# Moving batch 1's q loads ahead of a weight load, and turning q through the banks of the second channel matmul

## The chip, the cores and the metric

The kernel runs on one core of one Trainium2 chip. The metric is the device time of one execution in microseconds (us). Each run is labelled fast or slow: slow when it is over 1.5% above the fastest of its kernel, which comes with a lower granted TensorE clock. A ratio is the mean time of one kernel's fast runs over that of the other's of the same rounds, so it is not quite the ratio of the medians quoted beside it. It stands with its 95% interval.

## The reference

A linear attention with a cosine reweighting, then a mixer over tokens and one over channels; eight batches, 576 tokens, eight heads of 64.

```python
def phi(x, c, s):
    r = np.maximum(x, 0.0)
    return np.concatenate([r * c, r * s], axis=-1)
q_p, k_p = phi(q, cos_w, sin_w), phi(k, cos_w, sin_w)
kv  = np.einsum('bhsf,bhsd->bhfd', k_p, v)
num = np.einsum('bhsf,bhfd->bhsd', q_p, kv)
den = np.einsum('bhsf,bhf->bhs', q_p, np.sum(k_p, axis=2))[..., None] + 1e-06
x = (num / den)                                  # heads side by side: (batch, 576, 512)

xt = x.transpose(0, 2, 1)
u  = x + (np.maximum(xt @ w_tok1, 0.0) @ w_tok2).transpose(0, 2, 1)
return u + np.maximum(u @ w_ch1, 0.0) @ w_ch2    # 512 -> 1536 -> 512
```

## The kernel before

Inputs are loaded in float32, turned into bf16 features ("qfeat", "kfeat") and multiplied on TensorE. The q features have to be transposed ("turned") before they can multiply kv: either on TensorE through a PSUM bank (`qturn_mm`, `qturn_out`), or by a transposing DMA (`qturn_dma`). Likewise u is transposed for the first channel matmul (`mlp1`), whose result goes into the second (`mlp2`, twelve steps of k in three parts). In the names below, `num` multiplies the turned q features with kv, `x_out` divides that by the sum in its last column and so frees `num`'s bank (a bank is the piece of PSUM that a matmul writes), `b1` is the first token matmul, `u_mm` the second, and the tail is the last 64 of the 576 tokens. A "w_ch2 cast" turns a staged piece of the second channel weight into bf16. All tiles of SBUF are handed out one behind the other in the order in which they are named:

```python
raw = {n: [sb(f"{n}_raw{i}", [P, H, NJ, D], F32) for i in range(2)] for n in "qkv"}
# ... kp, qp, vb, qpT, kv_sb, x_sb, x_tl, x_tc ...
rden = [sb(f"rden{i}", [P, 2, HH], F32) for i in range(2)]
B1 = [sb(f"B1_{i}", [P, NT, Dm], BF16) for i in range(2)]
u_sb = [sb(f"u_sb{i}", [P, T, Dm], F32) for i in range(2)]      # also w_ch staging
u_tl = sb("u_tl", [P, B // 2, Dm], F32)                         # also w_ch staging
# ... u_bf, u_bt, uT, uTt, h1T (also w_tok staging), res (also w_ch staging), ...
```

Three places are changed. The head (batch 0) ends so:

```python
for c in (2, 3):
    uT_x(c, bank_u[c])
for c in (2, 3):
    uT_h(0, c, bank_u[c])                 # needs the relu of the second B half
    uT_out(0, c, bank_u[c], (A, V)[c - 2])
for mi in (0, 1):
    mlp1_part(0, mi, bank_h[mi], (0, 1))  # needs only uT blocks 0 and 1
```

The middle, between batch 0 and the loop, mixes batch 1's attention with batch 0's second channel matmul:

```python
wc2_load(0, SY)
load(1, q, "q", (SY, SY))
for i in (1, 2):
    wc2_load(i, SY)
# ...
for j in range(NJ):
    kv(1, j)
for t in range(3):
    p(0, t)                               # 12 matmuls of mlp2 part 0
for j in range(NJ):
    qfeat(1, j, V, A if j != 3 else V)
turn1(0, V)
turn1(1, A)
p(0, 3)
turn1(2, V)
turn1(3, A)
num1(0)
p(1, 0)
# ... num1 and p(1, ...) in turn, then b1, then p(2, ...)
```

The loop has a plan by steps for the batches that follow; in that of its first round:

```python
for n in range(2):
    put(13 + n, u_step, b, n)
    put(15 + n, uturn_step, b, n)                # u cast, transposing DMA
for j in range(3):
    put((12, 13, 15)[j], qfeat, f, j, A, A)
    put((12, 13, 17)[j], qturn_dma, f, j)        # transposing DMA of q
put(8, q_load, 4)
put(9, v_load, 4)
```

## Time and profile before

| | before |
|---|---|
| time, median of 3 runs | 262.38 us (261.79 to 262.49) |
| span of the profiled run | 259.7 us |
| TensorE busy | 248.5 us |
| VectorE, ScalarE, GpSimd busy | 190.2, 155.4, 101.0 us |

The lines on the bound, the gaps and the chain of waits are in the prediction. Two more views of this kernel are needed below. The first is TensorE's timeline behind kv of batch 1 (start, length, engine and line, operation, output and input, shapes, count): the channel matmul at 37.19 fills the time in which q is awaited, without a gap ahead of the first turn at 39.78.

```profile
35.97 1.38 PE L190 MATMUL psA<-vb,kp 128*128 128x65 bf16 x40
37.19 2.76 PE L337 MATMUL psM<-w_ch,h1T 128*128 128x512 bf16 x11
39.78 1.06 PE L176 MATMUL psA<-ident,qp 128*128 128x128 bf16 x16
```

The second is the DMA view of the stretch from 20 to 44 us, in which the staged weights and batch 1's inputs come in back to back: how many packets moved, how much, how fast.

```profile
DMA packets 6483, 9.37 MB, mean 390 GB/s; under 512 B 193, under 2 KB 4113, under 8 KB 6480
```

### The profile page before, as it was taken

Reading aid. Unit: us, or ns where it says so; the run is one execution under the profiler, and the core shown is the slowest. Engines: PE = TensorE matmul, PEld = TensorE weight load, DVE = VectorE, ACT = ScalarE, POOL = GpSimd, SP = SyncE. Lnnn points to the kernel's source line nnn. Section 1 sums busy time; section 2 is a strip of 40 time slices with the busy share of each in tenths; the row PEclk is TensorE's granted clock in tenths of the full one; section 3 lists DMA queues with packets and bytes.
Section 4 is the critical chain, followed back from the end, with each engine's and each line's share of the span. In section 5 each row is a group of like instructions: output and inputs, shape, how many; then the busy total and the mean of one; then the engine's idle time right before and its main releaser. Section 6 shows DMA issues by size and latency. Waiting matters only on the chain.

```text
span 259.7 us, 5679 instructions
## 1 busy us (share of the span) xinstructions
PE 248.5 (96%) x2098; PEld 157.7 (61%) x2110; DVE 190.2 (73%) x452; ACT 155.4 (60%) x259; POOL 101.0 (39%) x176
## 2 busy tenths in 40 slices
PE   7698999999999999999999999999999999999994
PEld 2465456455568545865596558755865576486483
DVE  5893767799989479949994999399939763653563
ACT  4663586885999458945883589357934443513510
POOL 5188467261007910392039303820381054044041
PEclk9999999999999999999999999999999999999999
DMA  6999999999999999999999997976290034004004
GB/s 192 368 372 390 390 388 386 332 257 260 302 356 214 182 341 354 180 224 297 350 184 186 375 282 153 192 256 120 66 232 36 0 81 180 4 0 156 8 0 163
DMA packets 79948, 57.18 MB, mean 220 GB/s; under 512 B 48177, under 2 KB 74929, under 8 KB 79921
## 3 DMA queue, kind: packets, MB, share of 16 engines
q1 hardware_dynamic: 76128, 47.26, 67.8%
q0 software_dynamic: 2560, 8.39, 9.5%
q10 hardware_dynamic: 1232, 1.18, 1.4%
q8 instruction: 16, 0.26, 0.4%
q14 instruction: 12, 0.09, 0.1%
HBM read 35.85 MB, written 9.44 MB: 174 GB/s over the span
## 4 chain that ended last, share of the span: by engine, by line
PE 63%; DMA 3%; DVE 2%; issue 1%; DVEq 0%
PE psM L319 26%; PE psM L386 24%; PE psA L239 4%; PE psA L257 3%; DMA qpT<-qp 3%; PE psA L214 2%; PE psA L190 2%; DVE qp L147 1%; PE psA L298 1%; PE psA L386 1%; DVE res L413 0%; DVE res L438 0%; DVE res L424 0%; DVE res L409 0%; DVE res L428 0%
## 5 line engine op out<-in xcount | busy, mean ns | idle before, releaser
L319 PE MATMUL psM<-uT,w_ch 128*128 128x512 bf16 x368 | 88.0, 379 | 0.6 <-DVE res L438 0.6
L331 ACT ACTIVATE h1T<-psM 128x512 bf16<-128x512 f32 x93 | 55.5, 597 | 39.7 <-PE psM L319 38.0
L404 POOL TENSOR_TENSOR res<-res,u_sb 128x256 f32<-128x256 f32 x42 | 32.2, 797 | 96.2 <-DVE res L409 95.8
L319 PEld LDWEIGHTS <-w_ch 128*128 128x128 bf16 x416 | 38.1, 98 | 40.4 <-issue 0.8
L386 PEld LDWEIGHTS <-h1T 128*128 128x128 bf16 x288 | 27.3, 98 | 5.8
L145 ACT ACTIVATE kp<-k_raw,sin_t 128x512 bf16<-128x512 f32 (+1 forms) x45 | 28.4, 669 | 1.2 <-DMA k_raw<-in_k_dram 1.2
L145 ACT ACTIVATE qp<-q_raw,sin_t 128x512 bf16<-128x512 f32 (+1 forms) x40 | 26.6, 681 | 0.1
L386 PE MATMUL psM<-w_ch,h1T 128*128 128x256 bf16 x192 | 25.0, 273 | 0.0
L163 POOL CAST vb<-v_raw 128x512 bf16<-128x512 f32 (+1 forms) x38 | 20.7, 588 | 11.0 <-DMA v_raw<-in_v_dram 10.6
L386 PE MATMUL psM<-w_ch_t,k_raw 128*128 128x256 bf16 x186 | 23.6, 273 | 0.0
L386 PEld LDWEIGHTS <-k_raw 128*128 128x128 bf16 x204 | 19.7, 98 | 5.0 <-issue 1.2
L214 PEld LDWEIGHTS <-qpT 128*128 128x128 bf16 x320 | 14.8, 98 | 10.3 <-issue 1.6
L361 DVE TENSOR_TENSOR k_raw<-h1T 128x512 bf16<-128x512 bf16 (+2 forms) x31 | 11.1, 360 | 12.3 <-ACT h1T L331 11.5
L230 DVE TENSOR_TENSOR x_sb<-psA,rden 128x512 bf16<-128x512 f32 x28 | 19.4, 691 | 1.0
L262 DVE TENSOR_TENSOR u_sb<-psA,x_sb 128x1024 f32<-128x1024 f32 x16 | 19.4, 1216 | 0.1
L147 DVE TENSOR_SCALAR kp<-k_raw,cos_t 128x512 bf16<-128x512 f32 (+1 forms) x40 | 17.5, 468 | 1.8 <-DMA k_raw<-in_k_dram 1.8
L147 DVE TENSOR_SCALAR qp<-q_raw,cos_t 128x512 bf16<-128x512 f32 (+1 forms) x37 | 16.2, 469 | 2.0 <-DMA q_raw<-in_q_dram 2.0
L226 DVE TENSOR_SCALAR rden<-psA 128x8 f32<-128x8 f32 x35 | 5.7, 164 | 15.4 <-PE psA L214 15.1
L257 PE MATMUL psA<-B,w_tok 128*128 128x512 bf16 x64 | 16.4, 379 | 0.0
L214 PE MATMUL psA<-kv_sb,qpT 128*128 128x65 bf16 x280 | 14.3, 193 | 0.7 <-DMA qpT<-qp 0.4
L239 PE MATMUL psA<-x_sb,w_tok 128*128 128x512 bf16 x49 | 14.0, 379 | 0.6 <-DVE x_sb L230 0.2
L200 ACT CAST kv_sb<-psA 128x520 bf16<-128x520 f32 x7 | 4.2, 603 | 16.7 <-PE psA L190 16.7
(139 smaller groups left out, 391.6 us busy)
## 6 DMA issues: line engine op xcount, KB each, us to landing
out_dram<-res POOLq DMA_DIRECT2D x32, 256.0 KB, 4.9
k_raw<-in_k_dram SPq DMA_DIRECT2D x7, 640.0 KB, 8.2
v_raw<-in_v_dram SPq DMA_DIRECT2D x7, 640.0 KB, 9.9
q_raw<-in_q_dram SPq DMA_DIRECT2D x7, 640.0 KB, 11.2
k_raw<-in_k_dram SPq DMA_DIRECT2D x7, 512.0 KB, 6.6
v_raw<-in_v_dram SPq DMA_DIRECT2D x7, 512.0 KB, 10.0
q_raw<-in_q_dram SPq DMA_DIRECT2D x7, 512.0 KB, 8.7
u_sb<-in_moe_w_ch_dram SPq DMA_DIRECT2D x2, 1024.0 KB, 10.3
```

Of the source, the lines that this page charges most:

```text
L145: eng.activation(out_ap, in_ap, AF.Relu, bias=0.0, scale=s)
L147: eng.tensor_scalar(out_ap, in_ap, scalar1=s, scalar2=0.0, op0=ALU.mult, op1=ALU.max)
L163: eng.tensor_copy(out_ap, in_ap)
L214: nc.tensor.matmul(dst, w, kv_sb[:, h, 0:E1], start=True, stop=True, skip_group_check=True)
L230: nc.vector.tensor_mul(dst.rearrange("p (g h d) -> p g h d", g=2, h=HH), n[:, :, :, 0:D], rb)
L239: nc.tensor.matmul(b1_ps[b][mi], w1[:, jw, mi * P:(mi + 1) * P], x, start=(j == 0), stop=(j == T))
L257: nc.tensor.matmul(ps[:, half, :], w2[:, ki, 2 * c + half, :], B1[b % 2][:, ki, :], start=(ki == 0), stop=(ki == NT - 1))
L262: nc.vector.tensor_add(u_sb[b % 2][:, 2 * c:2 * c + 2, :], ps, x_sb[:, 2 * c:2 * c + 2, :])
L319: nc.tensor.matmul(ps.rearrange("p (t k) -> p t k", k=P), wc1[:, ki, mi * P:(mi + 1) * P], src[:, :, ki, :], start=(ki == 0), stop=(ki == ...
L331: eng.activation(h1T[:, mi, :], ps, AF.Relu)
L386: nc.tensor.matmul(m[tt][:, tt, :], a[:, c, tt * P:(tt + 1) * P], w[:, c, :], start=(pr < 4 and c == 0 and (tt == 0 or own)), stop=(c == N ...
L404: G.tensor_add(c[:, t, :], s[:, t, :], u[:, t, :])
```

## The change

The intent: bring q in before the weights that are wanted later, turn q earlier through the banks that the second channel matmul owns anyway, and fill the wait for the head's last relu with matmuls that don't need it. One small piece moves a multiply from VectorE to ScalarE, and gets a small tile of its own for the reciprocals, so that it need not wait for the shared one. Lastly one transposing DMA of q goes from step 13 to 17 of the loop's first round. The diff, cut to its core:

```diff
     rden = [sb(f"rden{i}", [P, 2, HH], F32) for i in range(2)]
+    r_t = sb("rden_t", [P, 1, HH], F32)
     B1 = [sb(f"B1_{i}", [P, NT, Dm], BF16) for i in range(2)]
...
+        if eng is nc.scalar:                      # in x_half: the tail's multiply
+            for h in range(HH):
+                eng.activation(dst[:, 0, h, :], n[:, 0, h, 0:D], AF.Copy, bias=0.0, scale=r[:, 0, h:h + 1])
+            return
...
+    tail_b = psK[1].rearrange("p (g n) -> p g n", g=1)
+    num_half(1, pairs[2], tail_b)                 # ahead of the first B half
...
+    for mi in (0, 1):
+        mlp1_part(0, mi, bank_h[mi], (0, 1))
     for c in (2, 3):
         uT_h(0, c, bank_u[c])
         uT_out(0, c, bank_u[c], (A, V)[c - 2])
-    for mi in (0, 1):
-        mlp1_part(0, mi, bank_h[mi], (0, 1))
...
-    wc2_load(0, SY)
     load(1, q, "q", (SY, SY))
-    for i in (1, 2):
+    for i in range(3):
         wc2_load(i, SY)
...
-    for ki in (0, 2):
+    for ki in (0, 3):
         wc2_cast(ki, G)
...
-    for ki in (1, 3):
-        wc2_cast(ki, A)
-    kv_out(1, A)
...                                                # turn1 now writes the banks mps of mlp2:
-        qturn_out(j, qturn_mm(j), eng)
+        qturn_out(j, qturn_mm(j, mps[j] if j < 4 else nextA()[:, 0, :]), eng)
...
-    for t in range(3):
-        p(0, t)
-    for j in range(NJ):
-        qfeat(1, j, V, A if j != 3 else V)
+    qfeat(1, 0, V, V)
+    qfeat(1, 1, V, A)
+    kv_out(1, A)
+    qfeat(1, 2, V, A)
     turn1(0, V)
     turn1(1, A)
+    for ki in (1, 2):
+        wc2_cast(ki, V)
+    qfeat(1, 3, V, A)
+    turn1(2, V)
+    qfeat(1, 4, V, A)
+    num1(0)
+    p(0, 0)
...                                                # num, turn and p(0, ...) in turn; p(1, ...) around b1
-                put((12, 13, 17)[j], qturn_dma, f, j)
+                put((12, 17, 17)[j], qturn_dma, f, j)
```

More of the change, by code (lines that the diff above doesn't have):

```diff
@@ L170, in qturn_dma, with qturn_mm @@
                                     in_=qp[j].rearrange("p h a d -> p (h a d)"))
-    def qturn_mm(j):
-        ps = nextA()
-        t = ps[:, 0, :].bitcast(BF16).rearrange("p (h t) -> p h t", h=H)
+    def qturn_mm(j, bank):
+        t = bank.bitcast(BF16).rearrange("p (h t) -> p h t", h=H)
         for h in range(H):
@@ L502, in num_half, with x_half @@
                 num_mm(ps[:, i, h * E1:(h + 1) * E1], 0, HH * hf + h, j)
-    def x_half(hf, js, ps, b, stages=(0, 1, 2)):
+    def x_half(hf, js, ps, b, stages=(0, 1, 2), eng=None, slot=None):
         m = len(js)
         n = ps[:, 0:m, 0:HH * E1].rearrange("p g (h e) -> p g h e", h=HH)
-        r = rden[(js[0] // 2) % 2]
+        r = rden[(js[0] // 2) % 2] if slot is None else slot
         rm = r[:, 0:m, :]
@@ L731 @@
         num_half(1, pairs[i], num_b[i])
-    x_half(1, pairs[0], num_b[0], 0, (0,))
-    x_half(1, pairs[0], num_b[0], 0, (1,))
-    x_half(1, pairs[0], num_b[0], 0, (2,))
-    x_half(1, pairs[1], num_b[1], 0, (0,))
-    x_half(1, pairs[1], num_b[1], 0, (1,))
+    tail_b = psK[1].rearrange("p (g n) -> p g n", g=1)
+    num_half(1, pairs[2], tail_b)
+    for st in range(3):
+        x_half(1, pairs[0], num_b[0], 0, (st,))
+    for st in range(2):
+        x_half(1, pairs[2], tail_b, 0, (st,), slot=r_t)
+    for st in range(3):
+        x_half(1, pairs[1], num_b[1], 0, (st,))
     b1_half(0, range(NJ), psK[0], 0)
     b1_half_out(0, psK[0], 0, A)
+    x_half(1, pairs[2], tail_b, 0, (2,), A, r_t)
     for c in range(2):
         uT_x(c, psT[c])
-    num_half(1, pairs[2], num_b[2])
-    x_half(1, pairs[1], num_b[1], 0, (2,))
-    x_half(1, pairs[2], num_b[2], 0)
     for c in range(2):
@@ L823, in num1 @@
         x_out(1, j)
-    for t in range(3):
-        p(0, t)
-    for j in range(NJ):
-        qfeat(1, j, V, A if j != 3 else V)
+    qfeat(1, 0, V, V)
+    qfeat(1, 1, V, A)
+    kv_out(1, A)
+    qfeat(1, 2, V, A)
     turn1(0, V)
     turn1(1, A)
-    p(0, 3)
-    turn1(2, V)
-    turn1(3, A)
-    num1(0)
-    p(1, 0)
-    num1(1)
-    p(1, 1)
-    turn1(4, A)
-    num1(2)
-    p(1, 2)
+    for ki in (1, 2):
[5 more added lines that the diff above has]
+    p(0, 0)
+    turn1(3, A)
+    num1(1)
+    p(0, 1)
+    turn1(4, A)
+    p(0, 2)
+    num1(2)
+    p(0, 3)
     num1(3)
-    p(1, 3, (0, 3))
     num1(4)
-    t_sum(0)
     for bb in range(2):
         tail_copy(bb)
-    p(1, 3, (3, 4))
+    p(1, 0)
+    for mi in range(NT):
+        b1(1, mi)
+        b1_out(1, mi, (A, V)[mi])
+        p(1, 1 + mi)
+    t_sum(0)
     for j in range(2):
@@ L850 @@
         qturn_dma(2, j)
-    for mi in range(NT):
-        b1(1, mi)
-        b1_out(1, mi, (A, V)[mi])
     load(3, k, "k", (SY, SY))
@@ L859 @@
         load(3, src_of[n], n, (SY, SY))
+    p(1, 3)
     p(2, 0)
```

## The prediction

> **What bounds the kernel now.** I read the page first: busy shares, then the slices.
>
> ```profile
> PE 248.5 (96%) x2098; PEld 157.7 (61%) x2110; DVE 190.2 (73%) x452; ACT 155.4 (60%) x259; POOL 101.0 (39%) x176
> DMA  6999999999999999999999997976290034004004
> ```
>
> TensorE is busy for 248.5 of 259.7 us, so all that can be won without removing matmuls is 11.2 us of idle TensorE. Most of that lies before 15 us (11.05 busy of 15.00), which the change leaves alone. The change adds and removes no matmul; it can only move TensorE's gaps. The DMA row says that transfers are queued until about 156 us, so landing times matter too.
>
> Second, the timeline of TensorE alone, from 15 to 60 us, for the places where one row's last start does not run into the next row.
>
> ```profile
> 22.28 0.39 PE L545 MATMUL psN<-ident,x_sb 128*128 128x128 bf16 x4
> 23.23 0.39 PE L550 MATMUL psK<-w_tok,B 128*128 128x512 bf16 x1 [0.56 <-ACT B L539]
> ...
> 41.54 1.06 PE L176 MATMUL psA<-ident,qp 128*128 128x128 bf16 x16
> 42.93 0.40 PE L214 MATMUL psA<-kv_sb,qpT 128*128 128x65 bf16 x8 [0.34 <-DVE qpT L163]
> ...
> 48.54 1.02 PE L239 MATMUL psA<-x_sb,w_tok 128*128 128x512 bf16 x4 [0.19 <-DVE x_sb L230]
> ```
>
> In steady state one 512-column matmul issues every 0.216 us (1.03 us for four, less the 0.38 us that one takes, over three), a 128-column transpose every 0.056 us, a 65-column matmul every 0.030 us. With those steps the gaps are: about 0.3 us near 19.7, 0.5 near 22.5 to 23.2 (0.7 in the records; one record of that group is missing), 0.5 at 42.4, and 0.14, 0.35 and 0.18 between 45.5 and 49.6. That is near 2.0 us in all. From 24 to 36 us TensorE has none.
>
> Third, the chain of waits that ended last, where it meets the loop over the later batches:
>
> ```profile
> 85.26 0.61 DVE res L438
> 85.87 0.12 issue
> 85.98 1.35 PE psM L319 x6
> 87.33 7.04 DMA qpT<-qp
> 94.37 0.05 issue
> 94.42 0.42 PE psA L214 x8
> ```
>
> After 94.42 the chain is TensorE almost without a break to the end. So the end is set by when TensorE gets past two stops: 0.7 us before 85.98 (last start before it 85.24) and 0.55 us before 94.42, where batch 3's last q block is awaited from a transposing DMA. The profile gives the first stop to the VectorE add at L438, but that reads another bank than the one this first matmul writes (the source rotates four banks; bank one was read at 83.98). The view of tile uT from 74 to 96 us has a better candidate:
>
> ```profile
> L272 SPq DMA_TRANSPOSE uT<-u_bf x2: 1238/1292/1347, 81.4 to 82.8; - x2
> DMA to landing us min/median/max: 3.1/3.4/3.6
> ```
>
> The second of these is issued at 82.8 and lands 3.1 us later or more: 85.9, which is when TensorE starts. I take the transposed u, not the add, for the releaser.
>
> [...]So swapping two loads on SyncE's queue swaps their landings and adds no bytes. The trace agrees: loads are issued about 11 us before they land, one behind the other (q's halves 11.2 us median between 17 and 45 us, at 389 GB/s). [...]The trace has 0.71 us for 512 columns with a pointer scale[...]. [...]512 columns take 0.69 us from PSUM and 0.48 or 0.42 from SBUF.[...]
>
> **The change, part by part.**
>
> *Tail x of batch 0 (near 18 to 21 us).* The four tail matmuls move ahead of the first B half: they delay it by 4 x 0.030 = 0.12 us, and the ScalarE relu behind it (19.30 now) and the first u matmuls (19.95 now) by the same. Two small VectorE instructions (0.16 and 0.18) move ahead of x of pair 1, which has slack: it lands near 20.3, needed at 21.2. The 0.42 us multiply on VectorE becomes four ACTIVATEs of 64 columns[...]. Their bank is wanted again at 21.1. So +0.12 us and no win here.
>
> *First channel matmul ahead of the last u matmuls (22.5).* Four 512-column matmuls, 4 x 0.216 = 0.86 us, go where TensorE waits for the relu, whose halves are done near 23.3. They cover the 0.5 us gap whole. The copies of the last two u blocks (0.6 and 0.69 us) then have 0.86 us of matmuls to hide behind instead of 1.73, and just fit. Net of the 0.12: TensorE reaches the next stage **0.4 us** earlier.
>
> *q before w_ch2, and the turns.* q(1) lands at 38.1 now. A w_ch2 part is 1.05 MB, 2.6 us at 389 GB/s. So q lands near 35.5 and w_ch2's first part at 38.1. VectorE can use q only behind its last relu of the first channel matmul (36.25 to 36.94 now, 0.4 earlier then). Going through VectorE in its order: relu to 36.55; four features at a step of 0.40 to 38.1; first turn copy 0.69 to 38.8; two w_ch2 casts to 39.6; feature, turn copy, feature to 41.1; five x_out of 1.05 to 1.13 each to about 47.1. TensorE against it: kv ends 36.8, then nothing until q block 0 is ready (37.4): 0.65 idle. Turns to 38.8; first num at 38.85; channel matmul part 0 waits for the casts (0.35 idle, two pieces); turn 3 waits for its features (0.2); turn 4 needs the bank that x_out(0) frees at 42.1 (0.35); num 4 waits for x_out(2) (0.3). After it the b1 matmuls are interleaved with the second part, which covers most of the old 0.53 there. I get part 2 starting near 51.05 against 50.87 now: idle of 1.6 in place of 1.0. So this part *gives back* **0.6 us**: the old order had 12 independent channel matmuls (2.6 us) to run behind kv while q was awaited, the new one has none.
>
> *The transposing DMA of batch 3's block 1 from step 13 to 17.* It is issued at about 78.4 now and holds SyncE to 81.29, although u's first half is cast at 79.1. Behind the u transposes instead, u goes out at 79.1 and 81.3, and lands near 84.5, before TensorE wants it (85.24). The first stop, **0.7 us**, goes. The q blocks follow back to back from 82.6, four at 1.3 us, the last issued near 86.7 (87.33 now), before or beside the four output stores that start at 85.82. It should land 0.3 to 0.8 us earlier, but it is wanted 0.7 + 0.55 us earlier. I count **0.3 us** of the second stop as won.
>
> Sum: -0.4 + 0.6 - 0.7 - 0.3 = -0.8 us.
>
> **Rivals.** (a) *The middle is as good as its intent:* no idle behind kv, all 1.0 us of old gaps gone. For it: q is 2.6 us earlier and no turn waits for DMA any more. Against it: VectorE's queue, 10.5 us of work from 36.55 to 47.1 without a hole. It would make -0.4 - 1.0 - 1.0 = -2.4, so 260.0. (b) *Everything before 94.42 is absorbed by the DMA:* if the last q transpose lands at 94.4 again, what TensorE wins earlier becomes a longer wait there, and the time stays 262.4. For it: DMA is queued through 95 us, and earlier transposes took up to 7.0 us to land. Against: the u transposes landed within 3.1 to 3.6 us of issue, so the queue is short there. (c) *VectorE becomes the bound in the middle more than I have it:* each slip in its chain counts whole; 1 us more there gives 262.6. (d) *The w_ch2 load hides nothing:* its first part lands at 38.1, first wanted at 39.1, so a late landing by over 0.5 us stalls part 0. Slower by over 2% would need 5 us of new TensorE idle; only a serialisation that I have not seen gives that.
>
> **Range and chances.** From 262.38 I take 0.8, and a little more for (a), since ScalarE and VectorE work freed from the wait for q may be used better than my walk has it: 261.4 us. The spread is (a) at 260.0, (b) and (c) near 262.5; the runs of before spread 0.7. 8 in 10: 260.4 to 262.5. Over 2% is 5.2 us, more than the sum of all gaps after 15 us: faster 0.01, same 0.97, slower 0.02.
>
> **What would show it right or wrong.** The gap before the last u matmuls is gone, and TensorE starts the loose u matmuls of psA (27.34 now) near 26.95. q features start at 36.5 on VectorE, no wait for q's DMA; w_ch2's first cast near 38.1. TensorE idles 0.5 us or more behind kv and part 2's first matmul is at 50.5 to 51.5. The first matmul of batch 2's channel step starts without the 0.7 us stop. The num of batch 3's block 4 still waits, if briefly, for its DMA. The prediction is wrong if the middle has under 0.5 us of idle, or if the u transpose is not what ended the first stop (then it stays, with L438 ahead of it), or if block 4 of q lands later than 94.

From the trace of before: the 0.71 us is that of an ACTIVATE on ScalarE, the 0.69 and the 0.48 or 0.42 us are VectorE's. The cut estimate for the tail x on ScalarE was only the argument that it ends before its bank is wanted again at 21.1; in the trace after, the four ACTIVATEs take 0.93 us and end at 21.05.

## The result, and the profile after

The changed kernel takes 265.38 us at the median of four runs (fast ones 265.08, 265.29 and 265.46; one slow run of 270.29). Before, with one more run, is at 262.09. The ratio is 1.0128 [1.0088, 1.0167]: slower by 1.3%, inside the 2% band, but 2.9 us above the upper end of the predicted range. The profiled runs, both fast, are 261.47 (before) and 265.29 (after).

The page's busy row of the kernel after shows where the loss is not: VectorE, ScalarE and GpSimd are as busy as before to 0.3 us. TensorE shows 2.0 us more for the same 2098 matmuls. Its ends are modelled, and a wait inside a row can count as busy: kv's 40 matmuls take 1.54 us below and 1.38 before.

```profile
PE 250.5 (95%) x2098; PEld 157.9 (60%) x2110; DVE 190.5 (72%) x453; ACT 155.1 (59%) x261; POOL 101.1 (38%) x176
```

I cut both traces at points that every variant has and took the time between them. "Head" runs from the first turn on TensorE to the first u matmul of L257; the next part from there to kv of batch 1 is 8.63 us in all kernels; "middle" runs from kv of batch 1 to the loop; "rounds 1, 2" are the loop's first two rounds, in which stop one and stop two of the prediction lie; "rest" runs to the last matmul.

| us | first turn at | head | middle | rounds 1, 2 | rest |
|---|---|---|---|---|---|
| before | 7.80 | 19.54 | 21.24 | 55.85 | 142.74 |
| after | 8.02 | 19.01 | 23.32 | 56.45 | 143.69 |
| difference | +0.22 | -0.53 | +2.08 | +0.60 | +0.95 |

The differences sum to the 3.32 us between the two last matmuls. The first column varies from run to run (7.6 to 9.1 over all kernels) and lies ahead of the change.

**Head, as predicted.** TensorE's timeline of the kernel after: the channel matmuls at 22.71 fill the wait for the relu, and the u matmuls of L257 start at 27.03 (predicted 26.95).

```profile
22.71 1.03 PE L326 MATMUL psT<-uT,w_ch 128*128 128x512 bf16 x4
23.79 0.38 PE L554 MATMUL psK<-w_tok,B 128*128 128x512 bf16 x1
...
27.03 1.03 PE L257 MATMUL psA<-B,w_tok 128*128 128x512 bf16 x4
```

**Middle, much worse.** The same timeline behind kv; brackets give the idle time just before a row and what ended it. The first turn waits for q's features, turn 4 for the bank that x_out frees. The wait at 40.55 is put down to a DMA into u_sb, but that one lands only at 42.28; the first weight cast, on GpSimd from 39.63 to 40.50, ends just before 40.55, so I take that cast for the releaser.

```profile
35.66 1.54 PE L190 MATMUL psA<-vb,kp 128*128 128x65 bf16 x40
37.90 1.09 PE L176 MATMUL psM<-ident,qp 128*128 128x128 bf16 x16 [0.70 <-DVE qp L148]
39.20 0.62 PE L176 MATMUL psM<-ident,qp 128*128 128x128 bf16 x8 [0.21 <-ACT qp L146]
39.66 0.41 PE L214 MATMUL psA<-kv_sb,qpT 128*128 128x65 bf16 x8
40.55 1.13 PE L337 MATMUL psM<-w_ch,h1T 128*128 128x512 bf16 x4 [0.48 <-DMA u_sb<-in_moe_w_ch_dram]
...
43.61 0.61 PE L176 MATMUL psA<-ident,qp 128*128 128x128 bf16 x8 [0.22 <-DVE x_sb L230]
```

Part 2 starts near 52.64 (eight steps of 0.216 behind 50.91), outside the 50.5 to 51.5 that the prediction named.

**Stop one gone, stop two grown.** Later in that timeline: round 2 starts at 87.05 with no wait. It is 28.07 us behind round 1's start, before it was 28.77, so the predicted 0.7 came. But two num groups, not one, now wait for q's transposing DMA, and longer.

```profile
87.05 2.75 PE L319 MATMUL psM<-uT,w_ch 128*128 128x512 bf16 x12
...
94.27 0.42 PE L214 MATMUL psA<-kv_sb,qpT 128*128 128x65 bf16 x8 [0.28 <-DMA qpT<-qp]
...
96.37 0.42 PE L214 MATMUL psA<-kv_sb,qpT 128*128 128x65 bf16 x8 [0.82 <-DMA qpT<-qp]
```

**Transfers are slower from the start.** The DMA view of 20 to 44 us of the kernel after has 372 GB/s where before had 390, though the queue was full in both (the DMA row of that stretch has the digit 9 in all 40 slices):

```profile
DMA packets 6031, 8.92 MB, mean 372 GB/s; under 512 B 177, under 2 KB 3584, under 8 KB 6028
```

In 24 us that is 0.45 MB less, or 1.2 us at that rate. Indeed q lands at 36.87 us where I had 35.5, and the first part of w_ch2 at 39.58 where I had 38.1. Nothing in the prediction's reasoning moves a byte more, so the question for the experiments is: why did transfers slow down?

**Theories.** (A) *Placement.* The tile `rden_t` takes 32 bytes per partition (16 of them used) ahead of B1, so all tiles behind it (u, res, h1T, transposed u, and the weights staged in them) start 32 bytes further on. I read the addresses out of the build: before, the DMA targets among them start at multiples of 256; after, all at 32 above one. That this slows the transfers was my supposition at this point; e1 to e3 test it. (B) *Order.* The new order of loads and of engine work makes the transfers collide, wherever the tiles lie. (C) *The middle is VectorE-bound* beyond what I had walked, and the DMA is a bystander.

My count of the trace's packets between 20 and 44 us, median nanoseconds by size:

```
              2048 B   1024 B   1280 B     start of B1, mod 256   raw q, k, v, mod 256
before          84       46       56              0                     192
after           88       49       60             32                     192
```

### The profile page after: what moved, and what is told of

Same layout as the page of the kernel before. It is cut to its first block, busy times and chain, and to the rows that moved or that the text cites. A ratio compares the mean times of both kernels' runs of the same rounds, so it can differ in the third digit from the quotient of the medians.

```text
span 263.2 us, 5683 instructions
## 1 busy us (share of the span) xinstructions
PE 250.5 (95%) x2098; PEld 157.9 (60%) x2110; DVE 190.5 (72%) x453; ACT 155.1 (59%) x261; POOL 101.1 (38%) x176
## 4 chain that ended last, share of the span: by engine, by line
PE 51%; DMA 3%; DVE 1%; ACT 1%; issue 0%; ACTq 0%
PE psM L319 24%; PE psM L386 18%; DMA uT<-u_bf 3%; PE psA L239 3%; PE psA L257 3%; PE psA L214 2%; PE psA L190 1%; ACT u_bf L267 1%; PE psA L386 1%; ACT kp L146 0%; PE psA L298 0%; DVE u_tl L303 0%; DVE res L413 0%; DVE kp L148 0%; DVE res L409 0%
## 5 line engine op out<-in xcount | busy, mean ns | idle before, releaser
L319 PEld LDWEIGHTS <-w_ch 128*128 128x128 bf16 x416 | 38.0, 97 | 41.1 <-issue 1.4
L257 PE MATMUL psA<-B,w_tok 128*128 128x512 bf16 x64 | 16.4, 379 | 0.0
L245 ACT ACTIVATE B<-psA 128x512 bf16<-128x512 f32 x13 | 7.8, 597 | 14.0 <-PE psA L239 13.9
L214 PE MATMUL psA<-kv_sb,qpT 128*128 128x65 bf16 x280 | 14.3, 193 | 1.2 <-DMA qpT<-qp 1.1
```

Source lines behind the costliest of these rows:

```text
L214: nc.tensor.matmul(dst, w, kv_sb[:, h, 0:E1], start=True, stop=True, skip_group_check=True)
L257: nc.tensor.matmul(ps[:, half, :], w2[:, ki, 2 * c + half, :], B1[b % 2][:, ki, :], start=(ki == 0), stop=(ki == NT - 1))
L319: nc.tensor.matmul(ps.rearrange("p (t k) -> p t k", k=P), wc1[:, ki, mi * P:(mi + 1) * P], src[:, :, ki, :], start=(ki == 0), stop=(ki == ...
```

## The experiments

Line numbers in views of edited kernels are off by the lines added. Times are medians of all runs in us, slow ones included, this kernel's first, then those of before in the same rounds.

### Placement alone

**e1: the kernel before, with an unused tile of 32 bytes ahead of B1.**

```diff
+    sb("pad", [P, 8], F32)
     B1 = [sb(f"B1_{i}", [P, NT, Dm], BF16) for i in range(2)]
```

> The kernel before with nothing changed but an unused 32-byte tile ahead of B1, so that B1, u_sb, u_tl, u_bf, uT, uTt, h1T and res start 32 bytes later, as they do in the changed kernel (there the new tile rden_t does it). Theory A (the shift slows DMA into and out of these tiles): q of batch 1 lands over 1 us later than 38.05, w_ch2's 2048-byte packets take 87 to 89 ns where they took 84, and the time is 263.3 to 265. Theory B (the shift costs nothing, the changed kernel loses by its new order alone): 262.1 within 0.6, q lands at 38.0 within 0.4.

Measured: 265.21 against 262.88, 1.0116 [1.0055, 1.0178]. One tile that nothing reads or writes costs, within the noise, what the whole change costs. (One of the four runs, 267.79, has a clock of 0.990; without it, and without before's 264.11 at 0.993, the ratio of the means is 1.0098.) The engines are as busy as before (VectorE 189.9 us, ScalarE 155.7, GpSimd 100.8), so it isn't they that the shift slows. The DMA view of the same stretch matches the kernel after, and so do the packets (88, 48, 60 ns):

```profile
DMA packets 6047, 8.92 MB, mean 372 GB/s; under 512 B 179, under 2 KB 3616, under 8 KB 6044
```

The view of waits (waiter, releaser: total, times, longest, us) of e1 shows where it surfaces in the loop: stop one is longer, not shorter.

```profile
PE psM L320 <- DMA uT<-u_bf: 1.6, 2, 1.5
PE psA L215 <- DMA qpT<-qp: 0.7, 1, 0.7
```

**e3: the same with 64 bytes**, to see whether it is the number 32 or the loss of the 256-byte start (`sb("pad", [P, 16], F32)`).

> As e1 with 64 bytes in place of 32: B1 and the tiles after it start at a multiple of 64, not of 256. If what matters is the 256-byte start, as slow as e1 (263.3 to 265 by theory A); if it is a 64-byte start, 262.1 within 0.6 with packets of 84 ns. Theory B: 262.1 in any case.

Measured: 265.92 against 262.88, 1.0120 [1.0083, 1.0157]; packets 88, 48, 60 ns. 64 is as bad as 32.

**e2: the kernel after, with 224 bytes behind `rden_t`**, so that B1 and all behind it start at multiples of 256 again.

```diff
     r_t = sb("rden_t", [P, 1, HH], F32)
+    sb("pad", [P, 56], F32)
```

> The changed kernel with 224 bytes of unused padding behind rden_t, so that B1 and all tiles after it start at a multiple of 256 bytes again. Theory A: 262.0 within 0.8, q of batch 1 lands near 35.5 and w_ch2's first part near 38.0, and the waits for transposed u at 115 and 194 us are gone. Theory B: 265.3 within 0.5, landings as in the changed kernel (36.87 and 39.58).

Measured: 263.84 against 262.88, 1.0013 [0.9967, 1.0058]; packets 84, 46, 59 ns; q lands at 35.75 and w_ch2's first part at 38.22, as theory A had it. All code of the change is in it, and by the ratio it is the kernel before again in time. Two points of theory A's text were missed: 263.84 lies above its 261.2 to 262.8 (before, too, ran 0.8 us longer in these rounds), and of the two waits for transposed u the one at 115 us is gone, the one at 194 still has 0.55. With e1: 1.0116 x 1.0013 = 1.0129, and the kernel after has 1.0128. So theory A holds for the bulk of the loss, and B doesn't explain it: the order is the same in e2, and e1 has the old one. The rate is back too:

```profile
DMA packets 6419, 9.30 MB, mean 388 GB/s; under 512 B 191, under 2 KB 4042, under 8 KB 6416
```

A caution: e2's trace is of a run of 263.98, the slowest of its three fast ones, while the profile of before is of a quick one (261.47). These two traces differ by more than the rounds do (the table below), so I take the sizes from the rounds and the places from the traces.

### The parts of the change alone

**e14: the head part alone**, on the kernel before: `mlp1_part` for banks 0 and 1 ahead of the last u matmuls.

```diff
+    for mi in (0, 1):
+        mlp1_part(0, mi, bank_h[mi], (0, 1))
     for c in (2, 3):
         uT_h(0, c, bank_u[c])
         uT_out(0, c, bank_u[c], (A, V)[c - 2])
-    for mi in (0, 1):
-        mlp1_part(0, mi, bank_h[mi], (0, 1))
```

> The kernel before with the head part alone, tiles where they were. The head wins 0.4 to 0.6 us at the first u matmuls. If the wait for q of batch 1 (it lands at 38.05 at the earliest, and the old middle starts its features with it) takes that up, the loop starts as before and the time is that of before, ratio 0.999 to 1.001. If it passes through: 0.998.

Measured: 262.17 against 262.48, 0.9981 [0.994, 1.0023], not clear of the noise by itself. The trace has it in place: the head takes 18.99 us instead of 19.54.

**e15: the q transpose from step 13 to 17 alone** (`(12, 17, 17)` for `(12, 13, 17)`).

> The kernel before with the last part alone, the q transpose of batch 3's block 1 from step 13 to 17. By e4's profile: the first stop (0.7 us) goes, the second grows from 0.55 to 2.3 us: ratio 1.002 to 1.005. By e5 against e2 (it was 0.3 per cent slower to undo it): 0.996 to 0.998.

Measured: 263.05 against 262.48, 0.9995 [0.9948, 1.0041]. No change, to within half a per cent. By itself the move doesn't remove stop one, as these two lines of its waits show: the transposed u has to go out behind a q transpose that holds SyncE until 79.89, goes out at 79.98 and 83.05 and lands at 86.67, later than before (85.85).

```profile
PE psM L319 <- DMA uT<-u_bf: 1.2, 1, 1.2
PE psA L214 <- DMA qpT<-qp: 0.9, 1, 0.9
```

**e4: both of these together.**

> The kernel before with only two parts of the change, and no new tile: the first channel matmul ahead of the last u matmuls, and the q transpose of batch 3's block 1 from step 13 to 17. My walk of the kernel before gave 0.5 us for the first (without the tail's 0.12) and 0.7 to 1.2 for the second: 260.4 to 260.9. If early savings are absorbed by the wait for the last q transpose near 94 us: 262.1 within 0.4.

Measured: 262.38 against 262.88, 0.9974 [0.9937, 1.0011]. Its view of waits shows that stop one is down to 0.2 us, but the step change doesn't shorten stop two, which is 2.3 us here; so the forecast of 260.4 to 260.9 was missed:

```profile
PE psA L214 <- DMA qpT<-qp: 2.3, 1, 2.3
```

**e6: the middle part alone**, with the order of loads, the new turns and the new mix of matmuls from the change, and no new tile.

```diff
-    wc2_load(0, SY)
     load(1, q, "q", (SY, SY))
-    for i in (1, 2):
+    for i in range(3):
         wc2_load(i, SY)
...                    # turns, features, casts and p(...) as in the change
```

> The kernel before with the middle part alone: q loaded ahead of w_ch2, the new order of features, turns and channel matmuls. No new tile, so all tiles stay where they were. By my walk this part costs 0.6 us of TensorE idle before the loop; in e2 it cost 1.35 us from kv to the first matmul of the loop. If TensorE's time before the loop counts, 262.7 to 263.8 (ratio 1.002 to 1.006). If the DMA queue alone sets the stop near 94 us, the loop starts 0.6 to 1.4 us late and the time is that of before within 0.3.

Measured: 263.55 against 262.58, 1.0042 [0.9996, 1.0087]. In its trace the middle takes 22.21 us instead of 21.24, so about 1 us is given back.

The four parts alone multiply to 0.9981 x 1.0042 x 0.9995 x 1.0116 = 1.0134; the kernel after has 1.0128. Each factor is uncertain by 0.4 to 0.6%, the product by about 1%, so that the agreement is closer than the runs allow one to claim. It leaves no sign of a cost of the tail x on ScalarE, which was not run alone.

**e5: e2 with the step change undone.**

> The aligned changed kernel (e2) with the last part of the change undone: the q transpose of batch 3's block 1 goes back from step 13 to step 13's place ahead of the u transposes. Theory: the move makes the last two q transposes land later, among the output stores (94.05 and 96.00 in e2, 92.43 and 94.37 before), and so loses more at the second stop than the first stop gives. Then this is 0.5 to 1.2 us faster than e2: a ratio of 0.995 to 1.000 to the kernel before. Rival, my prediction's step: the move wins 0.7 to 1.0 us, so that this is slower than e2 by that: a ratio of 1.003 to 1.006.

Measured: 264.45 against 262.58, 1.0047 [1.0006, 1.0088]. Beside e2's 1.0013 this would speak for the step change, against e15 and e10 below. In e5's trace stop one is back with 1.8 us, where e2 has none. The intervals overlap, and I leave it open.

### Why the middle gives back more than predicted

VectorE's timeline in the middle, from e2, where loads come in time. The prediction had 0.4 us for each of the casts and the feature.

```profile
38.61 1.31 DVE L165 CAST w_ch<-res 128x512 bf16<-128x512 f32 x2
39.84 0.47 DVE L149 TENSOR_SCALAR qp<-q_raw,cos_t 128x512 bf16<-128x512 f32 x1
...
40.83 0.83 DVE L149 TENSOR_SCALAR qp<-q_raw,cos_t 128x512 bf16<-128x512 f32 x1
```

Two casts take 1.31 us together, and one feature 0.83 where its neighbour takes 0.47. GpSimd's timeline of the same kernel has its own casts just then:

```profile
38.27 1.36 POOL L165 CAST w_ch<-res 128x512 bf16<-128x512 f32 x2 [2.62 <-DMA res<-in_moe_w_ch_dram]
40.77 1.92 POOL L165 CAST w_ch<-u_sb 128x512 bf16<-128x512 f32 x3 [1.13 <-DMA u_sb<-in_moe_w_ch_dram]
```

In the trace of the kernel after, the same casts can be read one by one: VectorE's two take 429 and 839 ns, GpSimd's two beside them 871 and 802 ns, where GpSimd's ten weight casts of the kernel before, from 35 to 45 us, took 611 to 617. That each of the two engines stretches the other's casts was my supposition from this; e12 tests it for VectorE's.

**e12: e6 with GpSimd's two casts at 38 us on ScalarE**, to take that neighbour away (one look).

```diff
-    for ki in (0, 3):
-        wc2_cast(ki, G)
...
     qfeat(1, 2, V, A)
+    for ki in (0, 3):
+        wc2_cast(ki, A)
     turn1(0, V)
```

> One look, at durations: the middle part alone (e6) with the two w_ch2 casts that GpSimd makes beside VectorE's two given to ScalarE. In e2 VectorE's two casts took 0.56 and 0.82 us and one feature 0.83, each beside a GpSimd cast, where such instructions take 0.42 to 0.48 alone. If it is the overlap with GpSimd that stretches them, VectorE's two casts take 0.42 to 0.48 here; if they are slow for another reason (their source tile just written by DMA), 0.56 and 0.82 again.

Measured: 264.5 us in one run, whose state is unknown. VectorE's pair of casts took 1.11 us in e6's timeline:

```profile
38.97 1.11 DVE L163 CAST w_ch<-res 128x512 bf16<-128x512 f32 x2
```

In e12's it is down to 0.75 us:

```profile
39.33 0.75 DVE L163 CAST w_ch<-res 128x512 bf16<-128x512 f32 x2
```

So the stretching is shown to come from GpSimd's neighbouring casts. (e11 below shows it from the other side: its loads come earlier, GpSimd casts from 36.81 on, and there VectorE's casts take 0.41 us each but four of its features about 0.8.) The time in the middle stays at 22.24 us all the same: ScalarE is late with its features now, as TensorE's timeline of e12 has it.

```profile
41.56 0.62 PE L175 MATMUL psM<-ident,qp 128*128 128x128 bf16 x8 [0.81 <-ACT qp L145]
```

What the stretching costs can be read by laying the traces of the new order side by side (without the kernel after, where VectorE waits for late loads as well). "VectorE" is the time from its first q feature to the start of the first x_out, with the casts between them; the prediction's walk had 36.55 to 41.1 for it.

| us | VectorE | middle, above before's 21.24 |
|---|---|---|
| the prediction | 4.55 | 0.6 |
| e6 | 4.80 | 0.97 |
| e5 | 5.09 | 1.27 |
| e2 | 5.17 | 1.35 |
| e11 | 5.61 | 1.79 |
| e12 | 4.51 | 1.00 |

From e6 to e11 every tenth that VectorE takes longer makes the middle a tenth longer: the second column is the first less 3.82 or 3.83 each time. With the 4.55 of the walk that would be 0.73, so the walk's 0.6 was nearly right for the durations that it used. e12 alone departs from it, by the wait for ScalarE.

### Can the two stops be had by other means?

**e7: the kernel before, with batch 4's v load at step 21 of round 1 instead of 9**, so that fewer bytes are queued at the stops.

```diff
-            put(9, v_load, 4)
             put(20, k_load, 4)
+            put(21, v_load, 4)
```

> The kernel before with one load moved: v of batch 4, issued at step 9 of the first loop turn (lands 79.83 and 81.65), goes to step 21, behind the q transposes of batch 3 and the k load. Theory C (the two stops near 86 and 94 us are the DMA queue's: transposes stand in it behind 1.2 MB that nobody needs before 100 us): the q and u transposes land 2 to 3 us sooner, both stops shrink, 0.7 to 1.3 us faster: ratio 0.995 to 0.997. Rival: the transposes are paced by the features that ScalarE and VectorE make, then no change, or the late v load stalls its casts at 88 us and the time grows.

Measured: 270.08 against 262.58, four of six runs slow; the two fast ones give 1.0157 [1.0081, 1.0234]. The profiled run is a slow one (clock 0.987), so only large things are read from it. Round 1 does run without its stop (28.06 us), but the load now stands ahead of the next transposed u, at the start of round 3:

```profile
PE psM L319 <- DMA uT<-u_bf: 4.8, 2, 4.4
```

This is a miss: a load taken out of one wait's way is put in another's.

**e8: e7 with the head part, and part 2's first matmuls ahead of b1.** The edit adds the diff of e14 to that of e7 and moves `p(2, 0)` ahead of the b1 matmuls and the u matmuls behind `p(2, 1)`.

> A version meant to beat both kernels: e7, with the first channel matmul ahead of the last u matmuls (0.35 to 0.5 us in e4) and one quarter of the last part of the second channel matmul ahead of batch 1's b1 matmuls, so that it covers the 0.53 us in which they wait for x. No new tile. Theory C: without the queue's stops these 0.9 us pass through: 260.0 to 260.8, ratio 0.990 to 0.994. If another wait takes their place, as e7.

Measured: 268.32 against 262.58, 1.0204 [1.0161, 1.0248]. The same wait is there, 4.1 us. This profiled run counts as fast, but its clock of 0.986 is no better than e7's. In both traces the clock is full for some 100 us ahead of the wait, though, and is halved for 3.4 us only at its end or behind it (from 119.0 in e7, from 120.2 in e8), so that the lower clock isn't what made the wait. And e8's fastest run, 266.56 us at a clock of 0.997, is still slower than any of before.

**e9: the kernel before, with all DMA targets at multiples of 256.** Besides the tiles behind B1, which were already there, the raw q, k and v (192 above one) and the transposed q (64 above one) are moved.

```diff
+    sb("pad0", [P, 16], F32)
     raw = {n: [sb(f"{n}_raw{i}", [P, H, NJ, D], F32) for i in range(2)] for n in "qkv"}
...
+    sb("pad1", [P, 32], F32)
     qpT = sb("qpT", [P, H, NJ, P], BF16)
...
+    sb("pad2", [P, 16], F32)
     B1 = [sb(f"B1_{i}", [P, NT, Dm], BF16) for i in range(2)]
```

> The kernel before with 256 bytes of unused padding in three pieces, so that the q, k and v tiles (192 past a multiple of 256 until now), the transposed q (64 past) and, as before, B1 and what follows start at a multiple of 256. No other edit. Theory A carried on[...]: the 1024-byte packets of the raw loads fall from 46 ns to 42 to 44 and the 1280-byte ones from 58 to 54 to 56, q of batch 1 lands 0.7 to 2 us sooner, and the time falls by 0.5 to 3 us: ratio 0.989 to 0.998. Rival (only a start off 64 or only a write to the staging tiles costs; e3 speaks against it): 1.000 within 0.003.

Measured: 260.87 against 261.64, 0.9976 [0.9943, 1.0008]. The rate from 20 to 44 us is the best of the kernels so far:

```profile
DMA packets 6644, 9.52 MB, mean 397 GB/s; under 512 B 202, under 2 KB 4305, under 8 KB 6641
```

Packets of 1280 bytes went from 56 to 55 ns (58.6 to 55.3 in the mean), but those of 1024 bytes stayed at 46, where 42 to 44 had been expected. Which of the three pads does it was not separated, and 0.24% is not clear of the noise. In the trace both stops are gone without any edit to the transposes: rounds 1 and 2 take 54.57 us instead of 55.85.

**e13: e9 with the head part.**

> e9 (all tiles that DMA touches at multiples of 256) with the head part alone: the first channel matmul ahead of the last u matmuls. In e9 both stops near 86 and 94 us are gone, so the 0.4 to 0.6 us that this part wins at the head should pass through to the end if nothing else holds: e9's ratio less 0.0015 to 0.002. In e10 the move of the q transpose had brought back a wait of 1.1 us at the second stop, and so hidden it. If the wait for q of batch 1 takes it up again: e9's ratio.

Measured: **259.82** against 262.48, 0.9899 [0.985, 0.9949]. It beats both kernels. e9 and e14 alone would give 0.9976 x 0.9981 = 0.9957, so the 1.0% is on the lucky side: before's runs on this chip scatter from 261.11 to 265.01. TensorE's timeline of e13 passes both stops without a bracket (kv, round 2's start, the fourth and fifth num group):

```profile
84.42 0.89 PE L193 MATMUL psA<-vb,kp 128*128 128x65 bf16 x24
85.14 2.75 PE L322 MATMUL psM<-uT,w_ch 128*128 128x512 bf16 x12
...
91.92 0.41 PE L217 MATMUL psA<-kv_sb,qpT 128*128 128x65 bf16 x8
...
93.03 0.41 PE L217 MATMUL psA<-kv_sb,qpT 128*128 128x65 bf16 x8
```

**e10: e13 with the q transpose at step 17**, as in the change. (It was run before e13.)

> e9 with the two parts of the change that e4 had (first channel matmul ahead of the last u matmuls; q transpose to step 17). If alignment and these parts add up, e9's ratio less 0.003. If faster loads have already taken the waits that they take, e9's ratio.

Measured: 261.27 against 261.64, 0.9978 [0.9951, 1.0006]. Stop two is back:

```profile
PE psA L217 <- DMA qpT<-qp: 1.1, 1, 1.1
```

**e11: the kernel after, with all DMA targets at multiples of 256** (pads as in e9; the third is `[P, 8]`, as `rden_t` is there).

> The changed kernel with the same padding as e9 (8 fewer floats in the last piece, for its own tile). If the new order is worth the same at any load speed, e9's ratio plus 0.001 to 0.004. If its middle suffers from late q and w_ch2 most, it gains more from alignment than e9: ratio at or under e9's.

Measured: 262.89 against 261.64, 1.0046 [1.001, 1.0082]. With placement at its best the change loses about as much as its middle part alone in e6.

The parts of the time in these traces, one run each, cut as in the table above:

| us | head | middle | rounds 1, 2 | rest |
|---|---|---|---|---|
| e1, shift by 32 | 19.51 | 22.34 | 57.39 | 143.07 |
| e3, shift by 64 | 19.94 | 21.24 | 57.03 | 143.93 |
| e14, head alone | 18.99 | 21.26 | 56.67 | 142.73 |
| e6, middle alone | 19.61 | 22.21 | 55.82 | 142.74 |
| e2, after aligned | 18.99 | 22.59 | 56.57 | 143.45 |
| e5, e2 with the old step | 19.03 | 22.51 | 57.42 | 143.26 |
| e4, head and step | 18.97 | 21.57 | 57.40 | 142.74 |
| e15, step alone | 19.94 | 21.24 | 57.19 | 142.72 |
| e9, all aligned | 19.64 | 21.24 | 54.57 | 142.72 |
| e13, all aligned, head | 18.99 | 21.24 | 54.58 | 142.72 |
| e10, all aligned, head and step | 19.14 | 21.24 | 55.90 | 142.72 |
| e11, after, all aligned | 18.99 | 23.03 | 55.10 | 142.72 |

Read down the columns: the head is 19.0 to 19.1 with its part and 19.5 to 19.9 without. The middle is 21.2 to 21.6 in the old order with B1 in place, and 22.2 to 23.0 in the new. The shift by 32 alone makes it 22.34, that by 64 leaves it at 21.24: e3's first turn came 1.3 us late and its clock was halved from 10.9 to 14.3 (0.992 in the mean), so that TensorE came to q later (q landed 2.4 us behind kv's start there, 3.5 in e1, 2.1 before) and lost its time elsewhere. Rounds 1 and 2 have a floor of 54.6 that only full alignment with the old step reaches, and a scatter of over 1 us above it otherwise.

## Why the prediction was wrong

**The step that failed: that the loads keep their speed. The missing term is the new tile.** The prediction lists the tail x part as "So +0.12 us and no win here", and of the loads it says that swapping them "swaps their landings and adds no bytes". Both were taken to mean that transfers keep their speed. The part brought a tile that takes 32 bytes, and its place shifted every tile behind it off a 256-byte start. That term was not in the sum at all; e1 measured it by itself as 1.16%, and e3 as 1.20%: 2.3 to 3.0 us by the medians. That is most of the loss of 3.3; the 1 us that the middle gives back and the 0.5 us that the head wins make up the rest. That the shift costs this is shown by e1, e2 and e3. Why it does was not shown: packets of 2048 bytes take 88 ns instead of 84, and nothing in the traces says what the 4 ns are spent on. Which of the shifted tiles matter was not separated either.

**The head, -0.4 us: right.** The trace after has 0.53 us less, and of the kernels in the last table those with the part take 19.0 to 19.1 us and those without 19.5 to 19.9. e14 times it at 0.2%, which is not clear of the noise. The term of +0.12 us in it for the tail x was right as well: from the first turn to the head's first u matmul the kernel after takes 12.26 us (8.02 to 20.28) and before 12.15 (7.80 to 19.95). The four ACTIVATEs took 0.93 us together.

**The middle, +0.6 us: right in kind, too small.** The waits came where they were put: behind kv (0.59 us idle in e2, predicted 0.65), at part 0 of the channel matmul (0.53, predicted 0.35), ahead of turn 4 (0.74, predicted 0.35). e2's middle took 1.35 us more than before's, e6's 0.97. The mis-sized term is VectorE's "two w_ch2 casts to 39.6 [...] feature, turn copy, feature to 41.1": I used 0.4 us for each from a timeline in which GpSimd had been quiet, and in e2 the casts took 1.31 us as a pair and a feature 0.83. e12 shows GpSimd's casts to be the cause of the stretching, and the table behind it that the middle pays for it in full (one trace each). There is also a slip in the sum: the five idle times that the prediction lists add up to 1.85 us, not to the 1.6 that it went on with. Rival (c) named VectorE as bound but not this reason. In the kernel after, q and w_ch2 also land 1.4 and 1.5 us later than walked, and the middle takes 2.08 more.

**Stop one, -0.7 us: right in the kernel after, but not a property of the move alone.** Round 1 took 0.70 us less, with the transposed u issued ahead of the q blocks. Because of the late middle the round began 1.77 us later than before; counted from its start, u went out (80.89 and 83.06) and landed (86.56) within 0.3 us of the walk. The doubt about the profile's own releaser, the VectorE add, was borne out: in e14, e1 and e3 the profile names the transposed u for the same wait. But in e15, with the move alone and the round beginning near its old time, u landed at 86.67 and the stop grew to 1.2 us, and in e9 and e13 the stop goes without the move. What decides it (how full the queue is, I suppose) was not isolated, and that the 0.7 came true here is in part luck.

**Stop two, -0.3 us: wrong in sign.** The prediction said "It should land 0.3 to 0.8 us earlier". It landed at 96.33 instead of 94.37 in the kernel after (the prediction's own sign of being wrong, "later than 94", came true, though it was set so tight that before meets it too), and at 96.00 in e2, though it was issued 0.9 to 1.6 us later only. Behind the move, four q transposes instead of three stand among the output stores that the prediction itself put at 85.82 on; I suspect this, and e10 against e13 agrees (1.1 us of wait against none), but e5 doesn't. Whether the step change alone is worth anything on the old placement stays open.

**Also open:** why packets of 1024 and 1280 bytes, which go to the raw tiles that did not move, slowed as well (46 to 49 and 56 to 60 ns in the kernel after, 48 and 60 in e1), and why those of 1024 did not speed up in e9. And at the start of round 6 the kernel after waits for a transposed u that took 5.6 us to land (before: 4.3); e2 has 5.3 there, so placement behind B1 doesn't explain that one.

## What to carry to other kernels

Look at what a change does to the addresses of everything declared behind it: a 32-byte scratch tile ahead of large DMA targets cost more here (1.16% in e1) than all of the reordering could win, so put small tiles last, or pad each DMA target to a multiple of 256 bytes (the pad of e2 took the change from 1.0128 to 1.0013; starts 32 and 64 above a multiple were tried, 128 was not). When a part of a change seems to cost nothing, run it alone as a no-op before explaining the rest. And take an instruction's duration from a stretch of the trace in which the same neighbours are at work.
